# Batch 0 of a fused attention and MLP kernel: v loaded ahead of the tail of q, and batch 0's work put in another order

## The chip, the cores and the metric

The kernel runs on one core of one Trainium2 chip. The metric is the device time in microseconds (us) of one execution. Engines in the text: PE is TensorE (matmuls), DVE is VectorE, ACT is ScalarE, POOL is GpSimd, SP is SyncE, which only issues transfers here. SP's transfers go through one queue (q1 in the profile, hardware_dynamic), POOL's through another (q0, software_dynamic). POOL's may change the type on the way, and POOL writes their descriptors itself, so each issue takes it some time.

## What is computed

Eight batches of eight heads, 576 positions of 64 features: a linear attention whose queries and keys are cut at zero and multiplied by the cosine and the sine of an angle that grows with the position (here called a rotation), followed by an MLP with a quick GELU over the 4608 rows of 512.

```python
theta = np.pi / 2.0 * pos / S
phi = lambda x: np.concatenate([relu(x) * cos(theta), relu(x) * sin(theta)], axis=-1)
q_p, k_p = phi(q), phi(k)                              # [b, h, s, 128]
kv  = einsum('bhsf,bhsd->bhfd', k_p, v)
num = einsum('bhsf,bhfd->bhsd', q_p, kv)
den = einsum('bhsf,bhf->bhs', q_p, k_p.sum(axis=2)) + 1e-6
x   = (num / den).transpose(0, 2, 1, 3).reshape(4608, 512)
h   = x @ w_in                                         # 512 x 2048
out = (h * sigmoid(1.702 * h)) @ w_out                 # 2048 x 512
```

## The kernel before

Each batch goes through the same stages: rotate k and q (bf16 results kr, qn), form kv per head on PE (kv_mm), multiply q against it (num_mm), divide, turn the result so that features lie on partitions (x), then the two matrix products of the MLP: mm1 with w_in, GELU on ACT, mm2 with w_out, and the rows go out. mm1 of a batch makes 16 column blocks of 128 (fc 0 to 15), each over up to 512 tokens (the last 64 tokens of each batch are gathered and done apart).

The program writes out the order of each engine's work by hand (`tc.manual_schedule()`), so each engine runs its instructions in the order of the source, and waits only for what an instruction needs. The pools only hand out buffers: four PSUM buffers "mm", two double ones "at".

Batch 0 is special, since nothing lies ahead of it to hide its loads. Its 576 positions lie on partitions in nine slices j of 64 features (a partition holds nine positions, 64 partitions a head, two heads side by side). Its loads and their order (lines 64 to 67 and 157 to 162):

- SP: k in two pieces (slices 0 to 2, then 3 to 8), q in two (0 to 3, then 4 to 8).
- POOL: a small copy out of k's first piece, the gate of line 158, holds POOL until that piece has landed; then v in two halves of two head pairs each (cast to bf16 into vb), w_in's columns 0 to 511 and 512 to 1023. Later (lines 497 to 501), behind a second gate on v, w_in's columns 1024 to 2047, k of batch 1 and two parts of w_out; further on q and v of batch 1 and the rest of w_out.

The order of batch 0's work (lines 474 to 567), by the names of the helpers:

- idle (line 441) and a few further matmuls on zeros keep PE busy until there is something to do.
- trig (line 165) rotates one slice: a cosine and a sine instruction, 128 x 256 each, on DVE, ACT or POOL.
- ksum_mm (line 265) adds up k's rotated slices on PE; ksum_rows (272) copies the two rows of sums, and ksum_turn (276) turns them into a column of kvs.
- qturn_pe(c) (line 201) transposes two slices of rotated q on PE; qevac(c) (212) copies them to qT, on DVE or ACT.
- kv_mm (line 236) multiplies rotated k by v, half of the heads at a time; kv_evac (261) copies the result to kvs.
- num_half and div_half (289, 304) do the first 128 tokens in two halves of the heads; num_mm(c) and num_div(c) (322, 333) the further columns of 128 tokens. put_eps (298) adds the small constant. num_div is a reciprocal (inv, line 341) and a product (xn, line 343).
- x_half (313) and xturn_mm, xturn_evac (355, 362) turn the divided result and copy it to x, on ACT.
- x_first (line 534) multiplies the first 128 tokens by w_in for fc 0 to 3, in two steps over the features; x_part(c) (530) does the same for one further column block of 128 tokens; then GELU, and mm1(0, 4) and on. wcol (140) names the columns of w_in that one fc uses.

In the order of before, PE runs the k sums, the transposes of q's first two chunks, the turn of the sums, then kv_mm of the first half, and so on to x_part(1). fc 0 to 3 need w_in's first part, fc 4 to 7 its second, and fc 8 to 15 its last.

Of the kernel before, what the change touches and what calls it, by code (L numbers as in the profile page):

```python
# [19 lines left out]
def kernel(  # L20
# [35 lines left out]
    def src_of(src, b, i0=0, i1=NI):  # L56
        return src[b, 2 * i0:2 * i1].rearrange("(i hh) (p j) d -> (hh p) i (j d)", hh=2, j=NS)
# [3 lines left out]
    kf, vf = [t[:, 0:NI * S].rearrange("p (i e) -> p i e", i=NI) for t in (kf2, vf2)]  # L61
    vb = raw("vb", BF16)
    qf0 = qf[:, 0:NI * S].rearrange("p (i e) -> p i e", i=NI)
    for t, src, cut in ((kf, k, 192), (qf0, q, 256)):
        nc.sync.dma_start(out=t[:, :, 0:cut], in_=src_of(src, 0)[:, :, 0:cut])
        nc.sync.dma_start(out=t[:, :, cut:S], in_=src_of(src, 0)[:, :, cut:S])


    NP = NS + 5
# [42 lines left out]
    qn0 = qn.rearrange("p c h f -> p (c h f)")[:, 0:NS * NI * 128].rearrange(  # L112
        "p (j i f) -> p j i f", j=NS, i=NI)
    qT = one.tile([128, H, 640], BF16, name="qT")
    w_in_t = [one.tile([128, KC, n], BF16, name=f"w_in_{i}") for i, n in enumerate((512, 512, 1024))]
    w_out_sb = one.tile([128, FC, d_model], BF16, name="w_out_sb")
    nc.gpsimd.memset(vt[:, :, :, 64:66], 1.0)
    nc.gpsimd.memset(qT[:, :, S:640], 0.0)
# [17 lines left out]
    def load_win(i, f0):  # L136
        n = w_in_t[i].shape[2]
        nc.gpsimd.dma_start(out=w_in_t[i], in_=win_r[:, :, f0:f0 + n])

    def wcol(kc, fc):  # L140

        g, c = divmod(fc, 4)
        w = w_in_t[g][:, kc, :] if g < 2 else w_in_t[2][:, kc, ts(g - 2, 512)]
        return w.rearrange("p (f c) -> p f c", c=4)[:, :, c]

    def load_kv(b):
# [5 lines left out]
            load_chunks(vf2, v, b, nc.sync)  # L152

    def load_wout(g):
        nc.gpsimd.dma_start(out=w_out_sb[:, ts(g, 4), :], in_=wout_r[g])

    gate = const.tile([1, 4], F32)
    nc.gpsimd.tensor_copy(gate[0:1, 0:1], kf[0:1, 0, 0:1])
    for i in (0, 2):
        nc.gpsimd.dma_start(out=vb[:, i:i + 2], in_=src_of(v, 0, i, i + 2))  # L160
    load_win(0, 0)
    load_win(1, 512)


    def trig(dst, src, j, act=False, eng=nc.vector):

        i = src[:, :, ts(j, 64)]
        for cs, w in enumerate((cosw, sinw)):
            o = dst[:, j, :, ts(cs, 64)]
            if act is True or (act == "sin" and cs == 1):  # L170
                nc.scalar.activation(o, i, AF.Relu, scale=w[:, j:j + 1])
            else:
                eng.tensor_scalar(o, i, 0.0, w[:, j:j + 1], op0=MAX, op1=MUL)  # L173

    def chunk(t, c):
        if c < 4:
# [88 lines left out]
    def ksum_mm(j, first=False, last=False):  # L265

        if first:
            st["ks"] = pmm.tile([128, 512], F32, name="mm")
        nc.tensor.matmul(st["ks"][0:2], sel, kr[:, j].rearrange("p i f -> p (i f)"),
                         start=first, stop=last)  # L270

    def ksum_rows():
        st["row"] = small.tile([2, 512], BF16, name="row", bufs=1)
        nc.vector.tensor_copy(st["row"], st["ks"][0:2])

    def ksum_turn():
        for i in range(NI):
            nc.tensor.matmul(st["ks"][:, ts(i, 2)], st["row"][:, ts(i, 128)], ident[0:2, 0:2],
                             start=True, stop=True)
        nc.vector.tensor_copy(st["kvs"][:, :, :, 64].rearrange("p hh i -> p i hh"),  # L280
                              st["ks"][:, 0:8].rearrange("p (i hh) -> p i hh", hh=2))

# [30 lines left out]
    def x_half(b, a):  # L313
        ps, xn = nums.pop((0, a))
        o = ps[:, 264:392].bitcast(BF16)
        for k in range(2):
            nc.tensor.transpose(o[:, ts(k, 128)], xn.rearrange("p h e -> p (h e)")[:, ts(k, 128)],
                                ident)
        nc.scalar.activation(x_cols(b, 0)[:, 2 * a:2 * a + 2], o.rearrange("p (k t) -> p k t", k=2),
                             AF.Copy)  # L320

    def num_mm(c, eps_too=False):
        ps = pat.tile([128, 2, 512], F32, name="at")
# [25 lines left out]
    def x_open(b):  # L349
        x[b] = xpool.tile([128, KC, MT], BF16, name="xT")  # L350

    def x_cols(b, c):
        return x[b][:, :, ts(c, 128)] if c < 4 else xt[:, :, ts(b, 64)]
# [5 lines left out]
            o = ps[:, kc // 2, ds(264 + (kc % 2) * 64, 64)].bitcast(BF16)  # L359
            nc.tensor.transpose(o, xv[:, ts(kc, 128)], ident)  # L360

    def xturn_evac(b, c):
        ps = nums.pop(c)[0]
        n = 128 if c < 4 else 64
        i = ps[:, :, 264:392].bitcast(BF16).rearrange("p a (k t) -> p a k t", k=2)[:, :, :, 0:n]
        o = x_cols(b, c).rearrange("p (a k) t -> p a k t", a=2)
        nc.scalar.activation(o, i, AF.Copy)  # L367

    def xturn_dma(b, c):
        xn = nums.pop(c)[1]  # L370
# [70 lines left out]
    def idle(n, cols=512):  # L441
        w = pmm.tile([128, 512], F32, name="mm")
        for _ in range(n):
            nc.tensor.matmul(w[:, 0:cols], warm[:, 0:128], warm[:, 0:cols], start=True, stop=True)
# [26 lines left out]
        xturn_evac(b, 4)  # L471


    idle(9)
    for j in (0, 1):
        trig(kr, kf, j)
    trig(kr, kf, 2, act=True)
    for j in (3, 4, 5):
        trig(kr, kf, j)
    trig(kr, kf, 6, act="sin")  # L480
    for j in (7, 8):
        trig(kr, kf, j, act=True)
    for n, j in ((0, 0), (0, 2), (0, 1), (2, 3), (0, 7), (0, 4), (0, 8), (0, 5), (0, 6)):
        if n:
            for _ in range(n):
                nc.tensor.matmul(spare, warm[:, 0:128], warm, start=True, stop=True)
        ksum_mm(j, first=(j == 0), last=(j == 6))
        if j == 0:
            spare = pmm.tile([128, 512], F32, name="mm")
    kv_open(0, 2, 64)  # L490
    kv_open(2, 4, 64)
    for j in (0, 1):
        trig(qn0, qf0, j)
    for j in (2, 3, 4, 5, 7):
        trig(qn0, qf0, j, act=True)
    trig(qn0, qf0, 6, eng=nc.gpsimd)
    nc.gpsimd.tensor_copy(gate[0:1, 1:2], vb[0:1, 3, 0:1])
    load_win(2, 1024)
    load(kf, k, 1)
    load_wout(0)  # L500
    load_wout(1)
    trig(qn0, qf0, 8, eng=nc.gpsimd)
    ksum_rows()
    qturn_pe(0)
    qevac(0)
    qturn_pe(1)
    qevac(1)
    ksum_turn()
    kv_mm(0, 2, vb_rhs, 0, 64)
    kv_evac(0, 2, 64)  # L510
    qturn_pe(2)
    qevac(2, act=True)
    num_half_open()
    num_half(0)
    div_half(0)
    x_open(0)
    kv_mm(2, 4, vb_rhs, 0, 64)
    kv_evac(2, 4, 64)
    qturn_pe(3)
    x_half(0, 0)  # L520
    qevac(3, act=True)
    num_half(1)
    div_half(1)
    num_mm(1, True)
    num_div(1, True)
    num_mm(2, True)
    num_div(2, True)
    x_half(0, 1)

    def x_part(c):  # L530
        for fc in range(4):
            mm1_part(0, fc, c * 128, c * 128 + 128)

    def x_first(k0, fcs=range(4)):
        for fc in fcs:
            for kc in (k0, k0 + 1):
                nc.tensor.matmul(hp[fc][:, 0:128], wcol(kc, fc), x[0][:, kc, 0:128],
                                 start=(kc == 0), stop=(kc == KC - 1))

    for fc in (0, 1, 3, 2):  # L540
        hp[fc] = pmm.tile([128, MT], F32, name="mm")
    x_first(0, (0, 1, 2))
    xturn_mm(1)
    xturn_evac(0, 1)
    x_first(0, (3,))
    x_first(2)
    num_mm(3, True)
    num_div(3, True)
    xturn_mm(2)
    xturn_evac(0, 2)  # L550
    x_part(1)
    xturn_mm(3)
    xturn_evac(0, 3)
    x_part(2)
    x_part(3)
    for fc in range(4):
# [158 lines left out]
```

## Time and profile before

| | |
|---|---|
| median of 3 runs | 291.1 us (291.03 to 291.21) |
| the profiled execution | 291.12 us |
| its span | 289.4 us |
| granted PE clock | 1.00 |
| busy: PE, DVE, ACT, POOL | 282.1, 121.9, 128.0, 37.1 us |
| PE busy up to 11.02 us / 11.02 to 17.13 / 17.13 to 24.45 | 9.32 / 5.76 / 7.25 us |
| k's second piece landed | 6.42 us |
| q's two pieces landed | 7.9 and 9.8 us |
| v's two halves landed | 10.98 and 12.37 us |
| w_in's three parts landed | 14.91, 18.45 and 23.76 us |

The span is what the profile covers; about 1.7 us of the execution lie around it. All times of instructions are counted from the span's start. A landing is the issue's start plus its time to landing. In a timeline a row has a start, a duration, the engine, the line, the operation and the tiles; in the chain of waits, start, duration and what the chain went through. A matmul's end is modelled, and matmuls overlap, so a step on PE is best read from start to start.

### The profile page before, as it was taken

Reading aid. Unit: us, or ns where it says so; the run is one execution under the profiler, and the core shown is the slowest. Engines: PE = TensorE matmul, PEld = TensorE weight load, DVE = VectorE, ACT = ScalarE, POOL = GpSimd, SP = SyncE. Lnnn points to the kernel's source line nnn. Section 1 sums busy time; section 2 is a strip of 40 time slices with the busy share of each in tenths; the row PEclk is TensorE's granted clock in tenths of the full one; section 3 lists DMA queues with packets and bytes.
Section 4 is the critical chain, followed back from the end, with each engine's and each line's share of the span. In section 5 each row is a group of like instructions: output and inputs, shape, how many; then the busy total and the mean of one; then the engine's idle time right before and its main releaser. Section 6 shows DMA issues by size and latency. Waiting matters only on the chain.

```text
span 289.4 us, 5412 instructions
## 1 busy us (share of the span) xinstructions
PE 282.1 (97%) x2140; PEld 154.9 (54%) x2172; DVE 121.9 (42%) x323; ACT 128.0 (44%) x223; POOL 37.1 (13%) x69
## 2 busy tenths in 40 slices
PE   8999999999999999999999999999999999999995
PEld 2675646755555554555455545554555455554444
DVE  4834435772657266624670567148614300000000
ACT  6966644662146314631364126511760157761111
POOL 6683004100110011001100110001000100002000
PEclk9999999999999999999999999999999999999999
DMA  7999999999699899996999589967992610002322
GB/s 242 242 214 292 284 236 202 354 309 223 162 226 241 200 219 251 230 219 158 228 286 215 127 228 257 203 177 200 290 157 61 113 55 1 2 0 45 86 89 73
DMA packets 83545, 53.51 MB, mean 185 GB/s; under 512 B 57888, under 2 KB 78112, under 8 KB 83520
## 3 DMA queue, kind: packets, MB, share of 16 engines
q1 hardware_dynamic: 77456, 36.97, 57.2%
q0 software_dynamic: 6064, 16.19, 20.6%
q8 instruction: 17, 0.28, 0.4%
q14 instruction: 8, 0.07, 0.1%
HBM read 36.70 MB, written 9.44 MB: 159 GB/s over the span
## 4 chain that ended last, share of the span: by engine, by line
PE 92%; DMA 3%; ACT 2%; DVE 1%; issue 1%; ACTq 0%; POOL 0%
PE mm L432 42%; PE mm L383 37%; PE mm L411 4%; PE at L328 3%; DMA vb<-in_v_dram 2%; PE at L249 2%; PE at L241 1%; ACT g L388 1%; DMA kf<-in_k_dram 1%; PE at L360 1%; PE mm L404 1%; DVE xn L343 0%; PE mm L209 0%; ACT xT L367 0%; DVE xh L309 0%
## 5 line engine op out<-in xcount | busy, mean ns | idle before, releaser
L432 PE MATMUL mm<-w_out_sb,g 128*128 128x512 bf16 (+1 forms) x508 | 116.1, 372 | 1.2 <-issue 0.2
L383 PE MATMUL mm<-xT,w_in 128*128 128x512 bf16 (+1 forms) x582 | 112.1, 348 | 0.5
L388 ACT ACTIVATE g<-mm 128x512 bf16<-128x512 f32 x128 | 75.6, 598 | 32.5 <-PE mm L383 32.4
L383 PEld LDWEIGHTS <-w_in 128*128 128x128 bf16 x592 | 60.6, 113 | 48.7
L432 PEld LDWEIGHTS <-g 128*128 128x128 bf16 x528 | 48.8, 98 | 49.6
L436 ACT ACTIVATE ysb<-mm 128x512 f32<-128x512 f32 (+1 forms) x37 | 21.7, 586 | 111.2 <-PE mm L432 111.2
L439 POOL DMA_DIRECT2D out_dram<-ysb x36 | 19.7, 548 | 221.3 <-ACT ysb L436 221.3
L343 DVE TENSOR_TENSOR xn<-at,inv 128x512 bf16<-128x512 f32 x39 | 27.0, 691 | 1.3
L339 DVE TENSOR_SCALAR den<-at 128x8 f32<-128x8 f32 x36 | 6.0, 166 | 29.8 <-PE at L328 29.7
L328 PEld LDWEIGHTS <-qT 128*128 128x128 bf16 x312 | 14.4, 98 | 7.5
L189 DVE TENSOR_SCALAR qn<-qf,cosw 128x512 bf16<-128x512 f32 (+1 forms) x33 | 15.8, 478 | 3.9 <-DMA qf<-in_q_dram 3.9
L189 DVE TENSOR_SCALAR kr<-kf,cosw 128x512 bf16<-128x512 f32 (+1 forms) x25 | 12.0, 480 | 11.9 <-DMA kf<-in_k_dram 11.9
L328 PE MATMUL at<-kvs,qT 128*128 128x65 bf16 x312 | 15.8, 193 | 0.0
L189 DVE TENSOR_SCALAR qn<-qf,sinw 128x512 bf16<-128x512 f32 (+1 forms) x33 | 15.8, 478 | 0.0
L252 DVE CAST kvs<-at 128x520 bf16<-128x520 f32 x5 | 3.5, 702 | 27.3 <-PE at L249 27.3
L432 PE MATMUL mm<-w_out_sb,gt 128*128 128x512 bf16 x62 | 13.9, 379 | 0.1
L411 PE MATMUL mm<-xt,w_in 128*128 128x448 bf16 x64 | 12.3, 352 | 0.0
L173 DVE TENSOR_SCALAR kr<-kf,cosw 128x256 bf16<-128x256 f32 x24 | 9.0, 376 | 7.4 <-DMA kf<-in_k_dram 7.4
L189 DVE TENSOR_SCALAR kr<-kf,sinw 128x512 bf16<-128x512 f32 (+1 forms) x25 | 12.0, 479 | 0.0
L634 DVE CAST vt<-vf 128x2048 bf16<-128x2048 f32 (+1 forms) x10 | 7.9, 820 | 6.6 <-DMA vf<-in_v_dram 6.6
L432 PEld LDWEIGHTS <-gt 128*128 128x128 bf16 x64 | 6.3, 98 | 7.5
L413 ACT ACTIVATE gt<-mm 128x448 bf16<-128x448 f32 x16 | 8.7, 543 | 3.3 <-PE mm L411 3.2
(93 smaller groups left out, 129.3 us busy)
## 6 DMA issues: line engine op xcount, KB each, us to landing
qf<-in_q_dram SPq DMA_DIRECT2D x6, 1024.0 KB, 6.3
out_dram<-ysb POOLq DMA_DIRECT2D x24, 256.0 KB, 4.0
kf<-in_k_dram SPq DMA_DIRECT2D x5, 1024.0 KB, 6.9
vf<-in_v_dram SPq DMA_DIRECT2D x5, 1024.0 KB, 11.0
w_out_sb<-in_moe_w_out_dram POOLq DMA_DIRECT2D x4, 512.0 KB, 17.7
out_dram<-ysb POOLq DMA_DIRECT2D x12, 128.0 KB, 6.3
kf<-in_k_dram POOLq DMA_DIRECT2D x1, 1152.0 KB, 13.4
vf<-in_v_dram POOLq DMA_DIRECT2D x1, 1152.0 KB, 21.0
```

The source lines that it names most:

```text
L173: eng.tensor_scalar(o, i, 0.0, w[:, j:j + 1], op0=MAX, op1=MUL)
L189: nc.vector.tensor_scalar(o, i, 0.0, sc, op0=MAX, op1=MUL)
L328: nc.tensor.matmul(ps[:, h // 4, ds((h % 4) * 65, 65)], qT[:, h, ts(c, 128)], kvs_of(h), start=not eps_too, stop=(not eps_too or h % 4 == ...
L343: nc.vector.tensor_tensor(xn, pv[:, :, :, 0:64], inv.unsqueeze(3).to_broadcast([128, 2, 4, 64]), op=MUL)
L383: nc.tensor.matmul(hp[fc][:, t0:t1], wcol(kc, fc), x[b][:, kc, t0:t1], start=(kc == 0), stop=(kc == KC - 1))
L388: nc.scalar.activation(g, hp.pop(fc), AF.Gelu_apprx_sigmoid)
L411: nc.tensor.matmul(hps[:, 64:B * 64], wcol(kc, fc), xt[:, kc, 64:B * 64], start=(kc == 0), stop=(kc == KC - 1))
L413: nc.scalar.activation(gt[:, fc, 64:B * 64], hps[:, 64:B * 64], AF.Gelu_apprx_sigmoid)
L432: nc.tensor.matmul(yp[b, t, c0][:, c0:c1], w, w_out_sb[:, fc, c0:c1], start=(fc == 0), stop=(fc == FC - 1))
L436: nc.scalar.activation(ysb[:, c0:c1], yp[b, t, c0][:, c0:c1], AF.Identity)
L439: eng.dma_start(out=dst[:, c0:c1], in_=ysb[p0:p0 + n, c0:c1])
L634: nc.vector.tensor_copy(vt2[0:n, c0:c1, :, 0:64], i.rearrange("p (h c d) -> p c h d", h=H, c=c1 - c0))
```

## The change

The transfers: k of batch 0 goes out on SP in three pieces (slices 0 to 2, 3 to 5, 6 to 8), q's slices 0 to 3 behind it. q's slices 4 to 8 move to POOL's queue, behind v, in two pieces (4 and 5, then 6 to 8). w_in's columns 0 to 511 are loaded in two halves, with fc 0 and 1 in the first and fc 2 and 3 in the second; so these blocks take every second column of a half in place of every fourth, and w_out's first 512 rows are loaded in the rows' order that goes with it.

```diff
-    for t, src, cut in ((kf, k, 192), (qf0, q, 256)):
-        nc.sync.dma_start(out=t[:, :, 0:cut], in_=src_of(src, 0)[:, :, 0:cut])
-        nc.sync.dma_start(out=t[:, :, cut:S], in_=src_of(src, 0)[:, :, cut:S])
+    for t, src, c0, c1 in ((kf, k, 0, 192), (kf, k, 192, 384), (kf, k, 384, S), (qf0, q, 0, 256)):
+        nc.sync.dma_start(out=t[:, :, c0:c1], in_=src_of(src, 0)[:, :, c0:c1])
...
-    w_in_t = [... for i, n in enumerate((512, 512, 1024))]
+    w_in_t = [... for i, n in enumerate((256, 256, 512, 1024))]
...
     def wcol(kc, fc):
+        if fc < 4:
+            return w_in_t[fc // 2][:, kc].rearrange("p (f c) -> p f c", c=2)[:, :, fc % 2]
...
     def load_wout(g):
-        nc.gpsimd.dma_start(out=w_out_sb[:, ts(g, 4), :], in_=wout_r[g])
+        o, i = w_out_sb[:, ts(g, 4), :], wout_r[g]
+        if g == 0:
+            o = o.rearrange("p (s c) d -> p s c d", c=2)
+            i = moe_w_out[0:512].rearrange("(s p c) d -> p s c d", s=2, c=2)
+        nc.gpsimd.dma_start(out=o, in_=i)
...
     for i in (0, 2):
         nc.gpsimd.dma_start(out=vb[:, i:i + 2], in_=src_of(v, 0, i, i + 2))
+    for c0, c1 in ((256, 384), (384, S)):
+        nc.gpsimd.dma_start(out=qf0[:, :, c0:c1], in_=src_of(q, 0)[:, :, c0:c1])
     load_win(0, 0)
-    load_win(1, 512)
+    load_win(1, 256)
+    load_win(2, 512)
```

The order of batch 0's work after the idle matmuls is new as a whole. Below, V, A and P are DVE, ACT and POOL; krig and qrig rotate one slice of k or q, cosine or sine; ksum_turn is split into its matmuls (ksum_turn_mm) and its copy (ksum_col); x_first(a, fcs) does features half a for the blocks fcs. Two copies move from ACT to DVE: that of x_half for the first half of the heads and that of the third column block (`act=False`).

```diff
+    krig(V, 1, COS); krig(A, 0, SIN); krig(V, 0, COS); krig(A, 1, SIN); krig(V, 2, COS); krig(A, 2, SIN)
+    krig(V, 3, SIN); krig(A, 5, SIN); krig(V, 4, SIN); krig(A, 3, COS); krig(V, 5, COS); krig(A, 4, COS)
+    krig(V, 6, SIN); krig(A, 6, COS); krig(V, 7, SIN); krig(V, 8, SIN); krig(A, 8, COS); krig(V, 7, COS)
+    for n, j in enumerate((0, 1, 2, 3, 5, 4, 6, 8, 7)):
...
+        ksum_mm(j, first=(n == 0), last=(n == 8))
+    kv_open(0, 2, 64); kv_open(2, 4, 64)
+    qrig(V, 0, SIN, COS); qrig(A, 2, COS, SIN); qrig(V, 1, COS); qrig(A, 1, SIN); qrig(V, 3, SIN, COS)
+    qturn_pe(0); ksum_rows(); kv_mm(0, 2, vb_rhs, 0, 64); qevac(0, act=True)
+    ksum_turn_mm(); kv_evac(0, 2, 64); ksum_col()
+    qturn_pe(1); kv_mm(2, 4, vb_rhs, 0, 64); qevac(1)
+    num_half_open(); num_half(0); kv_evac(2, 4, 64)
+    qrig(A, 4, SIN); qrig(P, 5, COS); div_half(0); qrig(A, 5, SIN); qrig(A, 4, COS)
+    num_mm(1, True); num_div(1, True)
+    qrig(P, 7, COS); qrig(A, 6, SIN, COS)
+    nc.gpsimd.tensor_copy(gate[0:1, 1:2], vb[0:1, 3, 0:1])
+    load_win(3, 1024); load(kf, k, 1); load_wout(0); load_wout(1)
+    qrig(P, 8, COS, SIN)
+    qturn_pe(2); num_half(1); x_open(0); qrig(V, 7, SIN)
+    xturn_mm(1); qevac(2, act=True); div_half(1); x_half(0, 0)
+    qturn_pe(3); x_half(0, 1); num_mm(2, True); qevac(3)
...
+    x_first(0, (0, 1)); x_first(1, (0, 1)); xturn_evac(0, 1); num_div(2, True)
+    x_first(0, (2, 3)); x_first(1, (2, 3))
+    num_mm(3, True); xturn_mm(2); xturn_evac(0, 2); num_div(3, True)
+    x_part(1); xturn_mm(3); xturn_evac(0, 3, act=False); x_part(2); x_part(3)
```

(Several calls of the source stand on one line here.) Everything from the GELU of fc 0 on is as before.

## The prediction

> **What bounds the kernel now.** I read the engine table first, then the chain of work that ended last (whole, and its pieces up to 17 us in order of time), then what the change touches there: the transfers by stretch of time, and the timelines of DVE, POOL and PE.
>
> ```profile
> PE 282.1 (97%) x2140; PEld 154.9 (54%) x2172; DVE 121.9 (42%) x323; ACT 128.0 (44%) x223; POOL 37.1 (13%) x69
> PE 92%; DMA 3%; ACT 2%; DVE 1%; issue 1%; ACTq 0%; POOL 0%
> ```
>
> TensorE is the bound: 97% busy, 92% of the chain. The 3% of DMA all lie ahead of the first real matmuls of batch 0:
>
> ```profile
> 0.80 3.49 DMA kf<-in_k_dram
> 4.29 0.05 issue
> 4.34 0.13 POOL gate L158
> 4.47 6.51 DMA vb<-in_v_dram
> 10.98 0.04 issue
> 11.02 0.70 PE at L241 x36
> ...
> 14.79 0.70 DVE xn L343
> ...
> 15.97 0.61 ACT xT L367
> ```
>
> Columns: start, us, what. The chain is k's first piece, a gate on POOL, then v, which lands at 10.98; kv_mm (L241) starts at 11.02. From there to the first full column block of x (x_part(1), L383, at 17.13) PE works among short waits for DVE and ACT, and after 17.13 it is dense. So the time falls by as much as PE reaches 17.13 earlier, if nothing after that is late. Why v lands so late is seen in two stretches of the transfers (6.2 to 8.2 us, then 9.8 to 11.8):
>
> ```profile
> q1 hardware_dynamic: 636, 0.71, 109.3%
> ```
> ```profile
> q0 software_dynamic: 380, 0.41, 120.8%
> ```
>
> Columns: packets, MB, share. v's descriptors are done on POOL by 6.1 (timeline below), yet up to 8.2 only SP's queue (q1: k and q) moves data; v (q0) moves when q's tail, landed at 9.79 (2.40 + 7.4), is through. v waits for q's tail of 640 KB.
>
> **The change, part by part.** The sum is made against the profiled execution (291.12 us, span 289.4); the median of the runs is 291.1, so both agree to 0.02.
>
> *Transfers.* k's second piece (384 columns) is cut into two of 192; q's columns 256 to 576 leave SP and go out on POOL behind v, also in two pieces. SP's second and third k pieces land where the one did: 768 KB took 2.13 us (6.42 - 4.29), so 5.4 and 6.5, a little more for the smaller pieces (373 GB/s from 3.0 to 3.5, where 768-byte packets move, against 392 from 4.2 to 5.2 with 1536-byte ones). q's head took 1.49 after k (7.91 - 6.42): 8.0. Then v: its first half landed 1.19 after q's tail, its second 1.39 later; so 9.3 and 10.7, against 10.98 and 12.37. Then q's 256 KB: by the tail's 640 KB in 1.88 us it is 0.75; SP's queue has no row for 512-byte pieces, so from 0.75 to twice that; I take 0.8, as the 768-byte row lost only 5%: 11.5. q's last piece 12.5, w_in's halves 13.9 and 15.2 (w_in's first part took 2.54 whole; before 14.91). What was 768 KB ahead and 640 KB behind is only reordered, so w_in's last two parts land as before (18.45 and 23.76), later by 0 to 0.4 for the smaller pieces; I take 0.2.
>
> *v ahead.* kv_mm needs v, all k rotations and, in the new order, the first transposes. Rotations of k end at 8.0 on DVE (10 of them) and 7.7 on ACT (8 at a spacing of 0.40), before 8.8. The first transposes wait for ACT's third rotation of q (8.0 + 3 x 0.40 + 0.1 = 9.35) and take 0.23. kv_mm starts at 9.63, **1.39 earlier** than 11.02.
>
> *What is late next: DVE.* A DVE rotation is spaced 0.26, but while POOL writes descriptors one in each DMA takes 0.56:
>
> ```profile
> 4.66 0.35 DVE L173 TENSOR_SCALAR kr<-kf,sinw 128x256 bf16<-128x256 f32 x1
> 4.92 0.56 DVE L173 TENSOR_SCALAR kr<-kf,cosw 128x256 bf16<-128x256 f32 x1
> ...
> 7.20 0.56 DVE L173 TENSOR_SCALAR kr<-kf,cosw 128x256 bf16<-128x256 f32 x1
> ```
> ```profile
> 4.47 1.67 POOL L160 DMA_DIRECT2D vb<-in_v_dram  x2
> 6.12 1.53 POOL L138 DMA_DIRECT2D w_in<-in_moe_w_in_dram  x2
> ```
>
> The three long ones (4.92, 6.44, 7.20) all lie inside POOL's issues, and end about 0.1 after one of these; from 7.94, with POOL idle, all take 0.34. The change has seven DMAs there in place of four: 4.47 + 0.92 + 6 x 0.76, so until about 9.95. DVE's five rotations of q start at 8.06 and would end at 9.45; two long ones add about 0.5. So the row copy (L274, 0.67) ends at 10.62, not 10.04, and the turn of k's sums waits for it on PE: kv_mm ends 10.26, the turn starts 10.67, 0.4 idle. The Trainium skill, "SBUF — State Buffer", section "Who interferes with whom", calls the port pair that VectorE and GpSimd share an exclusive lock, which whoever comes second waits for the whole of; that speaks against this change. The trace agrees as far as it goes (0.56 for 0.35), and I take the measured 0.22 per DMA.
>
> *The rest of the way to 17.13.* The turn and the second transposes (0.17 and 0.46), which PE did ahead of v before, now lie behind it. kv_mm of the second half ends at 11.93, num_half(0) 12.2. num_mm(1) waits for the second kv copy (12.52): 12.7. Transposes of q's third chunk wait for ACT's three rotations of q's 256 columns, 11.54 + 3 x 0.40 + 0.1 = 12.83: start 12.88. xturn_mm(1) waits on DVE for xh (L309, 0.42), inv and xn (L343, 0.69): 14.05, idle 0.57. Then x_half(0), q's fourth chunk, x_half(1), num_mm(2) to 15.28; x_first, held 0.14 by x_half(1)'s copy, and num_mm(3) to 16.6; xturn_mm(2) 16.63; x_part(1) at 16.85. **The gain is 17.13 - 16.85 = 0.28**: 1.39, less 0.63 of moved PE work, less 0.48 for more waiting on DVE and ACT.
>
> *Edits at nothing.* The two copies moved from ACT to DVE (x_half(0), xturn(3)): the first lies beside PE's fourth transposes, the second (about 0.42 by L219's 512 columns) beside x_part(2) of 0.9 us; uncovered each costs its own time. w_out's first part in other rows: needed at 33.48, landed at 29.08. The strides in wcol: weight loads lie beside matmuls. POOL now rotates q ahead of the issue of w_in's last part: two rotations of 1.14 from 11.54, gate and issue at 13.9 in place of 12.55; behind it stand k of batch 1, w_out, q of batch 1. POOL's queue has work until about 16.6 (w_in's third part), and POOL's 256 KB output lands 4.0 us after its issue, so 13.9 is early enough.
>
> *What catches the gain.* w_in's last part is needed next:
>
> ```profile
> w_in<-in_moe_w_in_dram POOLq DMA_DIRECT2D x1, 1024.0 KB, 11.2
> ```
> ```profile
> 24.45 1.89 PE L383 MATMUL mm<-xT,w_in 128*128 128x512 bf16 x8
> ```
>
> It lands at 12.55 + 11.2 = 23.76, and mm1(0, 8) starts at 24.45. So of any gain only 0.65 less the transfers' own delay (0 to 0.4) can be kept. 0.28 fits. Later needs have more: v of batch 1 is copied by 42.3 and used at 44.0. Sum: 291.12 - 0.28 = **290.8 us**.
>
> **The rivals.**
> 1. *DVE is not held.* If the long rotations do not come (the descriptors of the small q pieces may be written in gaps), the row copy ends at 10.04, x_part(1) starts at 16.44 by the same sum: gain 0.65 and, with w_in's last part 0 to 0.1 later, 290.5 to 290.4. For it: in four DMAs only three rotations were long. Against: seven DMAs stand there.
> 2. *q's first piece on POOL lands late* (the other side). Up to 11.9 it hides behind the DVE chain; from 12.3 on the gain is gone, and from then one for one, since PE's third transposes stand in order ahead of all x work. At 13.2 (pieces of 512 bytes at half rate, 1.6 us, and one of the 16 engines 0.9 behind, as with w_in's second part: 17.41 for 15 of them, 18.45 for the last) it costs 0.9: 292.0.
> 3. *w_in's last part is late* by over 0.65: PE stands at mm1(0, 8) whatever was gained. At 1.5 (POOL's issue 1.35 later showing in full) it is 0.85 slower: 292.0. Against: the queue has other work until 16.6.
> 4. *v does not come earlier*, the change not doing what it says: with v at 10.98 and q's tail behind it x_part(1) starts at 18.0: 292.1. For it only that no row shows v without q ahead; against, the 4.0 us of POOL's outputs, since v's first half took 6.51.
> 5. *The queues share.* Then v would slow q's head by about 1 us (9.0), DVE and ACT would rotate q later, and x_part(1) comes at 17.4 to 17.5: 291.4. The Trainium skill, "DMA: Bandwidth & Descriptors", section "SWDGE vs HWDGE vs iDMA", says that each DMA engine goes round robin between the two kinds of queue; the stretch 6.2 to 8.2, with q1 alone, is against it.
>
> **How the numbers follow.** Forecast (290.5 to 291.1) 0.50; rival 1 0.20; rival 2 0.11; rival 3 0.08; rival 4 0.05; rival 5 0.06. A change of 0.2% (0.58 us) is about what a measurement of this kernel can tell from none. Faster than 290.5 holds most of rival 1 and a tail of the forecast: 0.24. Slower than 291.7 holds most of rivals 2, 3 and 4: 0.22. Within: 0.54. The range takes in the gain of rival 1 with nothing lost at w_in (290.2) and reaches to rivals 2 and 3 at most of their price: 290.2 to 291.8.
>
> **What would show it.** kv_mm's first matmul at 9.6 (v landed 9.3); long DVE rotations between 8.0 and 9.95 and the row copy ending near 10.6; PE idle ahead of the turn of k's sums, and about 0.6 ahead of xturn_mm(1); x_part(1) at 16.85; no wait at mm1(0, 8). Wrong would be: v still behind 10.5, q's 256 columns behind 12, or a PE wait for w_in's last part over 0.3.

## The result: slower by 0.3%, and the profile after

The changed kernel takes 292.46 us (median of 14 runs, 291.37 to 298.85); the kernel before took 291.15 in the same job (14 runs, 291.01 to 292.25). The ratio is 1.0032, 95% interval 1.0019 to 1.0045: slower by about 0.9 us. The ratio leaves out two disturbed runs of the change (296.25 and 298.85), so it is less than the quotient of the medians; without them the change's runs lie within 1.7 us of each other, before's within 1.2. Forecast were 290.8 and a range from 290.2 to 291.8: wrong in sign, and outside.

The profiled execution took 292.98 us (span 291.2; before 291.12 and 289.4). First the chain of work that ended last, in order of time (start us, us, what):

```profile
1.85 5.29 DMA kf<-in_k_dram
7.17 1.65 DVE kr L180 x4
8.82 1.25 DVE qn L180 x3
...
10.20 0.38 PE mm L220 x4
10.58 0.63 PE at L252 x36
...
14.97 0.18 POOL gate L568
15.15 0.22 POOL w_in L137
...
20.56 16.32 DMA qf<-in_q_dram
...
37.38 2.07 DVE qn L200 x5
39.45 4.70 SPq L234
...
44.33 6.39 DMA qT<-qn
```

v is gone from the chain. In its place stand k's third piece (1.85 + 5.29 = 7.14, forecast 6.5), DVE's rotations behind it, and then POOL: its rotations of q, the late issue of w_in's last part at 15.1 (forecast 13.9), the issues behind that, and q of batch 1, issued at 20.56 (17.84 before). PE's timeline in the front (start, us, engine, line, operation, count, idle before and what ended it):

```profile
7.87 0.38 PE L280 MATMUL mm<-kr,sel 128*2 128x512 bf16 x1 [0.46 <-DVE kr L180]
...
9.63 0.40 PE L220 MATMUL mm<-ident,qn 128*128 128x128 bf16 x4 [0.38 <-DVE qn L180]
...
10.52 0.70 PE L252 MATMUL at<-vb,kr 64*128 64x64 bf16 x36
...
13.85 0.62 PE L220 MATMUL mm<-ident,qn 128*128 128x128 bf16 x8 [0.40 <-ACT qn L178]
...
17.38 1.06 PE L402 MATMUL mm<-xT,w_in 128*128 128x128 bf16 x16
```

kv_mm (L252) is 0.50 earlier than before, not 1.39; x_part(1) (L402) is 0.25 later, not 0.28 earlier. That is a small part of 1.86. The rest comes between 41 and 51 us, where before had no such waits:

```profile
41.00 3.61 PE L451 MATMUL mm<-w_out_sb,g 128*128 128x512 bf16 x16 [0.21 <-DMA w_out_sb<-in_moe_w_out_dram]
44.86 1.26 PE L252 MATMUL at<-vt,kr 64*128 64x65 bf16 x72 [0.24 <-DVE vt L208]
46.59 1.02 PE L451 MATMUL mm<-w_out_sb,g 128*128 128x512 bf16 x4 [0.47 <-DMA w_out_sb<-in_moe_w_out_dram]
...
50.76 0.42 PE L344 MATMUL at<-kvs,qT 128*128 128x65 bf16 x8 [0.17 <-DMA qT<-qn]
```

Two of these steps in before, which started without a wait:

```profile
43.94 1.26 PE L241 MATMUL at<-vt,kr 64*128 64x65 bf16 x72
45.13 1.04 PE L432 MATMUL mm<-w_out_sb,g 128*128 128x512 bf16 x3
```

The four waits make 1.1. From start to start it is 1.57: the change is 0.24 behind before at its first mm2 matmul (33.72), 0.92 at 44.86, 1.46 at 46.59 and 1.81 at 50.76, and stays there. A wait is listed from the modelled end of the matmul ahead of it, so the listed ones are too short.

A transfer has landed when the last of its 16 transfer engines has (in before v's 16th at 10.98, and kv_mm at 11.02). Last landings, from the traces:

```
              before  forecast  change  change again
k, last part    6.42     6.5      7.14      6.82
v, first half  10.98     9.3      9.85     11.05
q 256-384        -      11.5     12.46     13.37
w_in, 2nd half   -      15.2     16.13     18.50
w_in, last     23.76    24.0     24.67     25.60
v of batch 1   41.06      -      44.02     42.84
w_out, last    43.55      -      46.55     45.36
```

("change again" is a second profiled execution, told below.) The first of the 16 has v at 9.10, and single engines come 0.3 to 2.5 us after the others, differently in each execution.

### The profile page after: what moved, and what is told of

It is laid out like the page before. It is cut to its first block, busy times and chain, and to the rows that moved or that the text cites. A ratio compares the mean times of both kernels' runs of the same rounds, so it can differ in the third digit from the quotient of the medians.

```text
span 291.2 us, 5448 instructions
## 1 busy us (share of the span) xinstructions
PE 283.3 (97%) x2172; PEld 152.9 (53%) x2172; DVE 123.5 (42%) x326; ACT 126.9 (44%) x220; POOL 39.6 (14%) x72
## 4 chain that ended last, share of the span: by engine, by line
PE 82%; DMA 10%; DVE 2%; SPq 2%; POOL 2%; issue 1%; ACT 0%; POOLq 0%; ACTq 0%; DVEq 0%
PE mm L451 38%; PE mm L402 33%; DMA qf<-in_q_dram 6%; PE mm L430 4%; PE at L344 3%; DMA qT<-qn 2%; PE at L260 2%; DMA kf<-in_k_dram 2%; SPq L234 2%; POOL qn L180 1%; DVE qn L200 1%; PE at L252 1%; DVE kr L180 1%; POOL w_out_sb L161 0%; DVE qn L180 0%
## 5 line engine op out<-in xcount | busy, mean ns | idle before, releaser
L451 PE MATMUL mm<-w_out_sb,g 128*128 128x512 bf16 (+1 forms) x528 | 117.7, 372 | 0.7 <-DMA w_out_sb<-in_moe_w_out_dram 0.7
L402 PE MATMUL mm<-xT,w_in 128*128 128x512 bf16 (+1 forms) x592 | 112.8, 349 | 0.0
L402 PEld LDWEIGHTS <-w_in 128*128 128x128 bf16 x592 | 59.0, 108 | 50.3
L180 DVE TENSOR_SCALAR kr<-kf,cosw 128x256 bf16<-128x256 f32 x23 | 8.0, 356 | 6.8 <-DMA kf<-in_k_dram 6.8
```

Of the source, the lines that this page charges most:

```text
L180: eng.tensor_scalar(o, i, 0.0, w, op0=MAX, op1=MUL)
L402: nc.tensor.matmul(hp[fc][:, t0:t1], wcol(kc, fc), x[b][:, kc, t0:t1], start=(kc == 0), stop=(kc == KC - 1))
L451: nc.tensor.matmul(yp[b, t, c0][:, c0:c1], w, w_out_sb[:, fc, c0:c1], start=(fc == 0), stop=(fc == FC - 1))
```

## The experiments

x_part(1) is its start in the profiled execution against that of before; ratios are to before in the same job.

```
run                ratio   95% interval      x_part(1)
order_alone        1.0026  1.0015 to 1.0037   +1.10
transfers_alone    1.0142  1.0120 to 1.0164   +3.98
after_again        1.0059  1.0047 to 1.0071   +2.38
k_two              1.0048  1.0027 to 1.0068   +0.92
w3_early           1.0035  1.0015 to 1.0055   +1.08
no_gate            1.0187  1.0153 to 1.0220   +6.11
lead_both          1.0234  1.0205 to 1.0264   +5.24
win_whole          1.0038  1.0021 to 1.0055   +1.91
before_late_issue  0.9993  0.9982 to 1.0004   +0.03
v_at_3             1.0141  1.0116 to 1.0167   +4.16
v3_w3early         1.0118  1.0084 to 1.0152   +2.04
v3_w3early_k2      1.0002  0.9986 to 1.0018   +0.60
before_k3          1.0082  1.0057 to 1.0108   +0.44
k2_w3early         1.0032  1.0018 to 1.0046   +0.76
good_transfers     1.0081  1.0068 to 1.0095   +2.50
row_first          1.0005  0.9995 to 1.0015   +0.08
row_first_x        1.0015  1.0004 to 1.0026   +0.26
row_first_xk       1.0019  1.0006 to 1.0031   +0.28
```

Two cautions. The rows come from five jobs, each on a chip of its own with before beside it: order_alone to k_two, w3_early to win_whole, before_late_issue to v3_w3early_k2, before_k3 to row_first, and the last two. The change itself, unedited, gave 1.0032 in the job of the result and 1.0059 in after_again, with intervals that don't meet, so a difference of 0.3% between rows of different jobs settles nothing. And in transfers_alone, no_gate, lead_both, v_at_3 and v3_w3early all executions but one or none have a granted clock of 0.982 to 0.994; the last section says what that costs.

My theory after the result: late landings, not the order, cost the time. Its rival: the new order costs it whatever the transfers do.

### Which half costs

order_alone is the changed kernel with before's transfers (k and q in two pieces on SP, w_in's first part whole); transfers_alone is before's order with the change's transfers; after_again is the change unedited.

```diff
 order_alone, against the changed kernel (transfers_alone is the reverse, against before):
-    for t, src, c0, c1 in ((kf, k, 0, 192), (kf, k, 192, 384), (kf, k, 384, S), (qf0, q, 0, 256)):
+    for t, src, cut in ((kf, k, 192), (qf0, q, 256)):   (two pieces each)
-    for c0, c1 in ((256, 384), (384, S)):
-        nc.gpsimd.dma_start(out=qf0[:, :, c0:c1], in_=src_of(q, 0)[:, :, c0:c1])
-    w_in_t ... enumerate((256, 256, 512, 1024))
+    w_in_t ... enumerate((512, 512, 1024))
...  (the loads of w_in and w_out and wcol to match)
```

> The new order of batch 0's work with the transfers of before (k in two pieces and all of q on SP, w_in's first 512 columns in one, w_out's first part as before). Transfer theory: the loss comes from the new transfers, which land later and later (w_in's last part 24.67 for 23.76, w_out's last part 46.55 for 43.55 in the changed kernel's profile) until PE waits for them at 41 to 51 us; with the old transfers those landings come back to within 0.4 us of before, no PE wait over 0.1 behind 40 us, and the time is that of before plus at most 0.6 (the new order wants v early and gets it at 10.98): 290.9 to 291.7, and a narrow spread of runs like before's. Order theory: the new order itself costs (POOL rotates ahead of the issue of w_in's last part at 15.1 for 12.55 and of q of batch 1 at 20.6 for 17.8): 292.0 or more, with the late landings still there.

> The new transfers with the order of work of before. Transfer theory: landings late as in the changed kernel (w_in's last part 24.5 or later, w_out's last 45.5 or later), PE waits behind 40 us, 292.0 to 293.0, wide spread. Order theory: like before in the batch 1 part, 291.0 to 291.5.

> The changed kernel once more, nothing changed, for a second profile and the spread. Both theories: 291.4 to 293.1 for most runs. Transfer theory: x_part(1) within 0.2 of 17.38 again, and the time of the profiled run follows the landing of w_out's last part one for one (46.55 at 292.98). Order theory: the landing of w_out's last part and the time do not move together.

Both halves cost, the transfers most, and their costs don't add up: 0.26% and 1.42% alone, 0.3 to 0.6% together. (Not all of the 1.42% is the clock: the one execution of transfers_alone at full clock took 294.24.) Each theory fails on one of them. Mine gave order_alone 291.7 at most, and it took 292.05 with no wait of PE behind 17 us; the rival gave transfers_alone 291.5 at most, and it took 295.34. I read it so that each half needs the other. order_alone's PE, ahead of kv_mm:

```profile
11.38 0.70 PE L244 MATMUL at<-vb,kr 64*128 64x64 bf16 x36 [0.79 <-DMA vb<-in_v_dram]
```

The new order has moved away the work that PE did while v came (the turn, the second transposes), so with v at 11.34 PE stands for 0.79. (0.36 of it is that v came later than in before: k's first piece, which lets POOL go on, had a late engine, 4.70 for 4.29.) In transfers_alone the old order wants all of q's rotations early, and q's 256 columns (12.81) leave PE idle for 1.61 ahead of the third transposes. after_again had other late engines than the first execution (v's 16th at 11.05, the 15th at 9.94; w_in's second half 18.50 against 16.00):

```profile
11.09 0.70 PE L252 MATMUL at<-vb,kr 64*128 64x64 bf16 x36 [1.02 <-DMA vb<-in_v_dram]
...
18.55 0.62 PE L507 MATMUL mm<-xT,w_in 128*128 128x128 bf16 x8 [1.14 <-DMA w_in<-in_moe_w_in_dram]
```

I had expected x_part(1) within 0.2 of 17.38; it came at 19.52. Here nothing is lost after 17 us (+2.38 there, +2.31 at the end), where the first execution lost most of its time. So in these two the loss falls where the latest engine meets PE, and one profile must not be read as the mechanism.

### w_in's last part

w3_early issues it right behind the third part, ahead of POOL's rotations. before_late_issue does the reverse to the kernel before. win_whole takes w_in's first part in one piece again.

```diff
 w3_early:           load_win(2, 512)
+                    load_win(3, 1024)   (from behind the gate on v)
 before_late_issue: +trig(qn0, qf0, 8, eng=nc.gpsimd)   (from behind load_wout(1))
                     nc.gpsimd.tensor_copy(gate[0:1, 1:2], vb[0:1, 3, 0:1])
                     load_win(2, 1024)
 win_whole:         -w_in_t ... enumerate((256, 256, 512, 1024))
                    +w_in_t ... enumerate((512, 512, 1024))
                    ...  (the loads of w_in and w_out and wcol to match)
```

> The changed kernel with w_in's last part issued right behind the third, at about 9.9 in place of 15.1 to 15.9. Lead theory (a POOL transfer whose turn comes within about 1.5 us of the end of its issue starts with packets of 0.3 to 1.2 us on some of the 16 transfer engines; the same packets take 0.1 where the lead is 2.5 us or more): no long packet of w_in's last part, its first and last landing at 22.0 to 22.7 and below 24.0 (23.0 and 24.7 in the changed kernel), the waits of PE behind 40 us gone; v's long packets stay. Since x_part(1) stays, 0.2 to 1.0 faster than the changed kernel in the runs that wait there. Engine-lag theory (some transfer engine is late by chance, whatever is issued when): the spread of w_in's last landing stays over 1.2 us. Concurrency theory (packets are long while POOL writes descriptors): v's packets get worse, since POOL writes up to 10.7.

> The kernel before, with one thing moved: POOL's rotation of q's last slice (2.3 us) runs ahead of the issue of w_in's last part, so that it is issued at about 14.9 in place of 12.55. Lead theory: its issue ends at 15.7, 0.9 to 1.2 ahead of its turn at 16.6 to 17; some 20 to 35 of its 512 packets take over 0.25 us (2 in before, none in the order alone), its landing is 24.5 to 25.2 in place of 23.76, PE waits 0.1 to 0.8 at mm1(0, 8) and the time rises by 0.1 to 0.8. Engine-lag theory (by chance): no more long packets than before, the time within 0.1 of before.

> The changed kernel with w_in's first 512 columns in one piece and w_out's first part as before. If the small pieces are what costs: w_in's landings 0.1 to 0.3 earlier and the time 0.1 to 0.5 lower. Lead theory: no change by over 0.3 in the median, except that the first blocks wait for the whole 512 columns, at 15.5 to 16.5; the long packets of v and of w_in's last part stay.

My "13.9 is early enough" was wrong about the transfer: of its 512 packets 2 took over 250 ns in before and 3 in w3_early, but 14 in before_late_issue (issued at 14.69), 27 in the change (15.10) and 30 in after_again (15.92). The shorter the lead of the issue over its turn on the queue (about 17), the more slow packets. But no run shows the time hanging on it. before_late_issue lost nothing: the part landed at 24.03, and PE takes it up at 24.48. (It doesn't delay q of batch 1, issued at 17.30, as the change does, 20.56 for before's 17.84.) And w3_early, whose profiled execution has no wait of PE behind 17 us at all, came out at 1.0035, no better than the change as far as two jobs tell; what that execution lost lies ahead of 17 us (+1.08). Taking back the cut of w_in won nothing either: in win_whole (1.0038) PE waited 1.33 for the whole first part, landed 17.57.

### v's issue, and k's cut

no_gate takes away the gate on k's first piece ahead of v's issue (v issued at 2.25, not 4.50); lead_both is that with w3_early; v_at_3 puts a memset there (issued at 3.25). k_two leaves k in two pieces; before_k3 is the kernel before with k in three. v3_w3early, v3_w3early_k2 and k2_w3early combine these; good_transfers is before's order with the transfers of v3_w3early_k2.

```diff
 no_gate: -nc.gpsimd.tensor_copy(gate[0:1, 0:1], kf[0:1, 0, 0:1])
 v_at_3:  +nc.gpsimd.memset(kr2[64:128, 4], 0.0)   (in the gate's place; from behind load_wout(3))
 k_two:   -(kf, k, 192, 384), (kf, k, 384, S), ...
          +(kf, k, 192, S), ...
 before_k3: the reverse, in the kernel before
```

> The changed kernel without the gate on k's first piece, so POOL issues v from about 2.3 in place of 4.5. Lead theory: v's descriptors are done by 4.0, 3 us ahead of their turn; no long packets of v, its first half lands at 9.2 to 9.5 on all 16 engines (9.85 and 11.05 in the two profiles), q's 256 columns at 11.6 to 11.9; x_part(1) at 16.6 to 17.0 and 0.5 to 1.5 faster than the changed kernel. With POOL done by 7.8, DVE's rotations of q are all 0.34 and those of k are lengthened. Rule of round robin between the two queues: v shares with k from about 3, k's second and third pieces land 1 us or more later (6.5 and 8.1), time 1 us slower than the changed kernel. Engine-lag theory: spread of v's landing stays over 0.7.

> Both: no gate, and w_in's last part issued behind the third. Lead theory: no long packets in v nor in w_in's last part, no PE wait over 0.2 behind 17 us, a narrow spread of the runs like before's, 290.6 to 291.2. Engine-lag theory: as the changed kernel, 291.4 to 293, wide spread. Round robin: k late, 292 to 294.

> The changed kernel with another gate: in place of waiting for k's first piece, POOL runs a memset of 0.95 us that it has to do anyway, so v is issued at about 3.25, after q's head on SP (2.4 to 2.9) and 1.2 earlier than with the gate. Lead theory: v's descriptors are done 2.2 us or more ahead of their turn at 7.0: no packet of v over 0.25 us, v's first half on all 16 engines by 9.5 to 9.7, q's 256 columns by 11.9 to 12.0, x_part(1) at 16.9 to 17.4; w_in's last part, issued at 14.4, with few long packets. Time 291.0 to 291.7. Sharing, as without a gate: v's packets move from 6 on beside q's head, which lands at 10 or later: 293 or more. Engine-lag theory: 291.4 to 293 as the changed kernel.

> The changed kernel with k in two pieces again (192 and 384 columns). Transfer theory: k's second piece lands at 6.4 to 6.6 in place of 7.14, q's head at 8.0 in place of 8.62, v's first half at 9.3, so x_part(1) starts 0.3 to 0.6 earlier, at 16.8 to 17.1; the later landings come 0.4 to 0.6 earlier and the time falls by 0.3 to 0.8 from the changed kernel's. Order theory: x_part(1) does not move by over 0.2, the time by less than 0.2.

> The same with w_in's last part issued behind the third. Lead theory: no long packet in v nor in w_in's last part, 290.6 to 291.4 and a narrow spread. Sharing: 293 or more. Engine-lag theory: 291.4 to 293.

> The same with k in two pieces too. Lead theory: k 0.3 earlier, 290.4 to 291.2. Sharing: 293 or more. Engine-lag theory: 291.4 to 293.

> The kernel before with one edit: k's second piece (384 columns) is cut into two of 192 on SP's queue, as the change does. Everything else is before's. Theory A, the smaller pieces alone make the last of the 16 engines late: k's third piece lands at 6.8 or later (6.42 before, 7.14 in the change), DVE's rotations end later than 8.81, time 291.3 to 291.6. Theory B, it needs v's transfer waiting right behind k and q's head (a shorter queue on SP): the third piece lands at 6.4 to 6.5 here, the second at 5.4 to 5.5, and the time is 290.9 to 291.2.

> The changed kernel with k in two pieces and w_in's last part issued right behind its third; v is issued behind the gate on k's first piece, as in the change. Theory A, v's early issue was not needed and the two pieces of k with the early issue of w_in's last part make the landings: v at 9.3 to 9.6, q's 256 columns at 11.9, w_in's last part at 23.7 to 23.9, and the time within 0.1% of before (291.1 to 291.5). Theory B, v has to be issued at 3.25 for that: v or q's 256 columns come 0.3 or more later, ratio 1.003 or more (292.0).

> Before's order of rotations, turns and divisions, with the transfers that came in time: k in two pieces, v issued at 3.25, q's last columns behind v on POOL, w_in's last part issued right behind the third. Theory A, before's order cannot use an early v: PE works on k's sums, the transposes and the turn until 10.9, so kv_mm starts at 10.9 to 11.0 whatever v does, gains at most 0.1, and the later q columns (11.7 for 9.8) hold the third transposes to 12.9: x_part(1) 0.3 to 1.0 later than before, time 291.4 to 292.1. Theory B, the early v is worth its 0.5 or more in any order: x_part(1) earlier than 17.13, 290.6 or less.

**With k in three pieces an earlier issue of v is harmful.** By the lead theory I expected a gain over the change from no_gate, lead_both, v_at_3 and v3_w3early; they are 1.2 to 2.3% slower than before. In no_gate both queues move data from 6.4 to 7.4 us, and together less than SP's queue alone did in before (351 GB/s from 6.4 to 7.8); columns of the first two lines are packets, MB, share, of the third us, busy times, granted clock, DMA share, GB/s:

```profile
q0 software_dynamic: 92, 0.11, 64.8%
q1 hardware_dynamic: 124, 0.12, 44.0%
```
```profile
6.40:7.40 1.00, 0.98 (x5) 0.17 (x3) 0.16 (x1) 0.48 (x2) 1.00 (x2) 1.00 1.09 227
```

That is what rival 5 feared, here in no_gate; in the change itself it hardly shows (v's first packet moves at 7.34, SP's last is done at 8.09). q's head then lands at 13.43, not 8.6, and PE waits 4.45 us for DVE's rotations of it. The Trainium skill, "DMA: Bandwidth & Descriptors", section "SWDGE vs HWDGE vs iDMA", says that each DMA engine alternates between the two kinds of queue. The trace agrees as far as it goes: 92 packets of one queue and 124 of the other in one microsecond, though not which engine moved which. In before, with SP's queue full up to 8.2, v's descriptors lay ready from 6.1 and did not move.

**Cutting k costs bandwidth.** before_k3 differs from before by this cut alone. Its transfers (4.2 to 5.4 and 5.4 to 6.4 us; last number GB/s), against 388 and 362 in the same stretches of before:

```profile
4.20:5.40 1.20, 1.20 (x4) 0.23 (x3) 1.03 (x4) 0.91 (x2) 1.08 (x3) 1.00 1.09 343
5.40:6.40 1.00, 1.00 (x3) 0.13 (x1) 1.00 (x4) 0.00 (x0) 1.00 (x2) 1.00 1.12 333
```

A 768-byte packet takes 38.7 ns (mean of 1496, without the queue's first 40), a 1536-byte one 67.5 (mean of 512, before): the same bytes take 15% longer. I charged 5%. k, then q's head, then v, all come 0.44 later on the first engine (v 10.91 for 10.47), and so does x_part(1). The Trainium skill, same page, section "Why small descriptors are slow (HBM only)", gives three cycles of overhead per packet beside one per 32 bytes: 2 x 27 against 51, an estimate of 6%. The measured 15% decides. k's third piece landed at 6.66, between what the two theories gave. Beyond this 0.44, two of before_k3's four runs (294.4) had a granted clock of 0.994, the two others took 292.0 and 292.6.

The cut decides most where v comes early: v3_w3early to v3_w3early_k2 is this edit alone, 1.0118 to 1.0002, intervals apart (and 293.0 to a median of 291.68 if of the first only the one execution at 0.999 of the clock is taken). With k in three, q's head had its 16th engine at 10.67 and the 1st at 7.82, and PE waited 1.88 us for it; with k in two it lands at 8.20 and v at 9.34, so there the issue of v at 3.25 does no harm; 2.25 was not tried with it. (In k_two, with w_in's last part issued late and v behind the gate, the cut shows no such difference: 1.0048 against 1.0059, intervals overlapping. Its profiled execution had late engines in both of k's pieces, 4.72 and 6.85, and x_part(1) at +0.92, where I expected it before 17.13.) Why a longer SP queue leaves single engines so late is open.

**Landings as forecast, and still no gain.** In v3_w3early_k2 v is at 9.34, q's 256 columns at 11.70, w_in's halves at 13.98 and 15.31, its last part at 23.54: the forecast's numbers within 0.5. x_part(1) was to be 0.28 early and is 0.60 late. k2_w3early has such landings too (9.21 and 11.53), but v's issue 1.25 later, so POOL writes descriptors up to 10.7, not 9.4, and DVE still has long rotations there:

```profile
9.52 0.82 DVE L181 TENSOR_SCALAR qn<-qf,cosw 128x256 bf16<-128x256 f32 x2
10.26 0.56 DVE L181 TENSOR_SCALAR qn<-qf,sinw 128x256 bf16<-128x256 f32 x1
```

Its row copy starts at 11.01, 0.50 after that of v3_w3early_k2, and PE stands 0.23 ahead of the turn for it: the forecast's DVE mechanism, and 0.16 at x_part(1). Their ratios, 1.0032 and 1.0002, come from two jobs and don't settle its price. In good_transfers such landings (v at 9.52) were worth nothing to before's order: kv_mm at 11.61, later than before's 11.02, since k's sums come late (k's last part at 6.78), and then 0.53, 0.40 and 0.78 of waiting for q's late columns.

### Mending the order

row_first is v3_w3early_k2 with DVE's chain ahead of the first transposes cut short; row_first_x also puts x_half(0) ahead of xturn_mm(1); row_first_xk moves one more rotation of k from DVE to ACT.

```diff
 row_first:
-    qrig(A, 2, COS, SIN)
-    qrig(V, 1, COS)
-    qrig(A, 1, SIN)
-    qrig(V, 3, SIN, COS)
+    qrig(A, 1, COS, SIN)
+    qrig(A, 2, COS, SIN)
     qturn_pe(0)
     ksum_rows()
+    qrig(V, 3, SIN, COS)
 row_first_x:
+    x_half(0, 0)   (from behind div_half(1))
     xturn_mm(1)
 row_first_xk:
-    krig(V, 7, COS)
+    krig(A, 7, COS)
```

> The kernel with k in two pieces, v issued at 3.25 and w_in's last part issued early, with one change of the order: ACT rotates q's slice 1 ahead of slice 2 (DVE no longer does its cosine), and the copy of k's sums stands on DVE ahead of q's slice 3. Theory A, DVE's chain (k's rotations to 9.05, three rotations of q, the row copy) is what holds the first transposes at 9.86 and kv_mm at 10.52: now the transposes start at 9.75 to 9.85, kv_mm at 10.2, x_part(1) 0.2 to 0.4 earlier than in the same kernel without it (17.73), time 291.2 to 291.5. Theory B, the hold is further down (DVE's inv and xn ahead of xturn_mm(1), 0.52 idle at 14.58): kv_mm earlier, but xturn_mm(1) still at 14.5 to 14.6 and the time that of the kernel without it, 291.7.

> The kernel that matched before (k in two pieces, v issued at 3.25, w_in's last part issued early, ACT on q's slice 1, the copy of k's sums ahead of q's slice 3), with one more edit: PE's two transposes of x_half(0) stand ahead of xturn_mm(1), where PE idled 0.43 for DVE's xn. Theory A, idle time of PE ahead of 17.2 is all that can be gained: x_part(1) 0.1 to 0.2 earlier (17.0 to 17.1), time 291.1 to 291.3. Theory B, DVE's copy of x_half now stands ahead of other work of DVE and gives the gain back at x_first: x_part(1) at 17.2 or later, 291.3 to 291.6.

> The same, and one rotation of k (slice 7, cosine) goes from DVE to ACT, which was done with k 0.5 us ahead of DVE. Theory A, DVE's end of k's rotations (9.08) holds the last sums and the first transposes: sums end 0.2 earlier, kv_mm at 10.2 to 10.3, x_part(1) another 0.1 to 0.2 earlier (16.8 to 17.0), time 290.9 to 291.2. Theory B, ACT becomes the late one (k's rotations on ACT end at 8.9, q's slice 1 at 9.7): kv_mm not earlier than 10.4, time that of the kernel without this edit or 0.1 to 0.3 more.

row_first brings x_part(1) from +0.60 to +0.08 and its median is 291.34 against 291.32: nothing of the change's loss is left, and nothing won. By the ratio there was none left without this edit either (1.0002, in another job), so in time the edit itself is not shown to be worth anything; in the traces kv_mm came only 0.1 earlier, and the rest was won behind it. PE's waits that are left in row_first, up to 60 us (us in all, times, longest):

```profile
PE mm L281 <- ACT kr L179: 1.0, 2, 0.7
PE at L377 <- DVE xn L360: 0.4, 1, 0.4
PE mm L221 <- DVE qn L181: 0.4, 1, 0.4
PE mm L281 <- DVE kr L181: 0.2, 1, 0.2
```

Halving the second (0.43 to 0.21, row_first_x) made PE wait 0.16 for the second xh instead, and the third transposes start 0.16 later; going at the last (row_first_xk) moved the late end to ACT. Neither beats before: theory B of both.

## Why the prediction was wrong

- *What bounds the kernel.* That PE bounds it held; that v's 6.51 us on the chain are what to shorten did not. PE's busy time from 7.3 to 17.13 us points to it, in before (first) and in the change:

```profile
sum 9.83, PE 9.04 PEld 6.60 DVE 8.14 ACT 8.31 POOL 7.32; mean PE 2.26 PEld 1.65 DVE 2.04 ACT 2.08 POOL 1.83
```
```profile
sum 9.83, PE 7.97 PEld 6.14 DVE 9.23 ACT 7.02 POOL 7.11; mean PE 1.99 PEld 1.54 DVE 2.31 ACT 1.75 POOL 1.78
```

  By this count PE had 0.79 us of idle time there in before, and 0.08 of it directly ahead of kv_mm: before's order had filled the wait for v with other work, and v at 9.52 won nothing with that order (good_transfers). The change made it 1.86, with DVE busier by 1.1; it reached x_part(1) only 0.25 later because more of k's sums were done by 7.3. The 0.79 is no upper limit: a matmul counts as busy to its modelled end (0.38 for 512 columns), and three in a row take 0.81 in the change (6.60), so PE had more room where k's sums came singly.
- *Transfers* is the step that failed. "A little more for the smaller pieces" was 15% and not 5%, and "5.4 and 6.5" for k was 5.48 and 7.14: of the 0.72 by which k's last part came later than in before, 0.42 is on the first of the 16 engines already (6.38 for 5.96), 0.30 on the last alone; "then v: 9.3" came at 9.85 and 11.05, "q's 256 KB: 11.5" at 12.46 and 13.37, "w_in's halves 13.9 and 15.2" at 14.7 to 15.6 and 16.1 to 18.5. I reckoned with a late engine of 0.9 only in rival 2. In the change q's 256 columns have the last engine 0.98 behind the first, and v's 0.75 (0.51 in before); in after_again v's last is 1.11 behind the 15th. Rival 2 (292.0, chance 0.11) is nearest to what happened: in its own place q's 256 columns hold the third transposes for 0.40, and late engines cost at other places too. The sign of being wrong that I had named, these columns behind 12, came.
- *v ahead.* "Rotations of k end at 8.0 on DVE" came at 8.81, 0.8 late (k's last piece 0.64 late, the rest long rotations), and the first transposes waited for DVE's third rotation of q (10.06), not for ACT's. kv_mm at 10.52 for 9.63. With k in two pieces (v3_w3early_k2) DVE ends at 9.05 and kv_mm is at 10.52 too, though v and q land as forecast: then the step fails for want of the earlier k. No run has k's pieces at 5.4 and 6.5, so whether the rest of the sum would have held with them is not shown.
- *What is late next: DVE.* Right in kind: the long rotations came where POOL writes descriptors, and the row copy ended at 11.16 (forecast 10.62). The 0.4 of idle time ahead of the turn did not come, since kv_mm was later still; PE stood ahead of the transposes instead (0.38 and 0.17). k2_w3early against v3_w3early_k2 shows them holding the turn for 0.23.
- *The rest of the way to 17.13* was charged too much: kv_mm to x_part(1) took 6.86 us, not 7.22 (6.11 in before). That x_part(1) missed by 0.53 only, after 0.89 at kv_mm, is luck.
- *Edits at nothing.* "13.9 is early enough" was wrong twice: POOL's rotations wait for q's late columns, so the issue was at 15.10, and a late issue has slow packets. At rival 3's place, mm1(0, 8), it cost next to nothing: the part landed at 24.67 and the step started at 24.71, by the starts held for about 0.1 (0.31 behind the transposes ahead of it, 0.22 in before).
- *What catches the gain.* "Later needs have more" put at nothing what cost most in the profiled execution: 1.57 of 1.86, from 41 to 51 us. POOL issued q of batch 1 2.72 later than before; v of batch 1 landed at 44.02 (41.06 before), w_out's last part at 46.55 (43.55), and PE waited for both. In w3_early and after_again PE has no such waits, and yet their profiled executions, 292.22 and 293.47, are not clearly faster.
- *Rival 4* came true in after_again for its own execution: v at 11.05, later than before. *Rival 1* did not: the long rotations came.
- Not foreseen: the parts do not add up. k's cut alone costs 1.0082, the order alone 1.0026, all transfers alone 1.0142, and together 1.0032 to 1.0059. I take it that late engines cost most where an order has no other work to cover them, but that is argued, not shown. What makes an engine late is open for k, v and q. For w_in there is one candidate: the queue of instruction fetches (q8) moves a packet of 16 KB in 0.97 us at 15.74 in before (0.95 at 15.27 in the change), about what the last engine of w_in's second part lags in before (0.94); on which engine, the trace does not keep. How the change's loss in the median divides between the front and the 41 to 51 us stretch is not settled: w3_early, free of the second in its profile, measures the same.
- Two slips of reckoning, without weight: 8.0 + 3 x 0.40 + 0.1 is 9.30, not 9.35; and 17.41 for w_in's second part holds for 14 of the engines, the 15th is at 17.51.

## What to carry to other kernels

As long as the order stays, a transfer that leads the chain of waits is worth about the bound engine's idle time beside it: read that stretch's busy sum first, since other work may already fill the wait. An order that takes this cover away needs its transfers on time on the last of the 16 engines, in every execution; look at more than one profile, and repeat the unedited kernel in each job before reading 0.3% out of two. Before cutting a transfer, divide packet time by bytes for the packet sizes involved.

## What was not expected of the hardware

In four traces long waits of PE in the front go with a stretch at half the granted clock (column before the last two; us, busy times ahead of it). no_gate, around PE's 4.45 us wait, and transfers_alone, whose longest single wait was 1.61:

```profile
14.30:18.00 3.70, 3.70 (x72) 3.02 (x74) 2.50 (x7) 3.00 (x8) 3.70 (x6) 0.50 1.33 192
```
```profile
14.30:17.80 3.50, 3.20 (x61) 2.98 (x62) 1.03 (x3) 1.98 (x5) 3.50 (x5) 0.51 1.18 185
```

lead_both (a wait of 3.55) and v_at_3 (2.15) have such a stretch of 3.4 us too. The length of one wait does not decide: v3_w3early waited 1.88 us at once and kept the full clock there. Five of after_again's six runs have a mean clock of 0.992 to 0.994, where 3.5 us at half clock would give 1 - 1.75/291 = 0.994; the sixth, the profiled one, has 1.0 and is no faster. So the clock can explain up to about 1.75 us of a run per such stretch, but not the change's loss: 11 of the change's 14 runs have a clock of 0.998 to 1.0, and all of them are above before's median.
